# Exchanging softmax statistics between partitions on VectorE instead of GpSimd, in a fused linear attention and MLP kernel

## The chip, the cores and the metric

The kernel runs on one core of one Trainium2 chip. The metric is device time in microseconds (us) of one execution, as the median of several. A core has a matrix engine (TensorE, PE), with weight loads as a second stream (PEld), and VectorE (DVE), ScalarE (ACT) and GpSimd (POOL), each of which works through its own queue in order. SyncE (SP) issues most DMAs here. Engines wait for each other through semaphores only.

## The reference

Eight batches of eight heads, 576 positions, 64 features. The queries are softmaxed over their 64 features, the keys over their 576 positions; a head's output is `q_s @ (k_s^T @ v)`. The heads are then joined to tokens and go through an MLP without bias.

```python
q_s = exp(q - max(q, axis=-1));  q_s = q_s / (sum(q_s, axis=-1) + 1e-9)
k_s = exp(k - max(k, axis=2));   k_s = k_s / (sum(k_s, axis=2) + 1e-9)
kv  = einsum('bhsd,bhse->bhde', k_s, v)
x   = einsum('bhsd,bhde->bhse', q_s, kv)   # joined to 4608 tokens x 512
h   = x @ w_in                             # 512 -> 2048
out = (h * clip(h + 3, 0, 6) / 6) @ w_out  # 2048 -> 512
```

Inputs and output are float32; the two MLP weights come as float64.

## The kernel before, in words

The 4608 tokens are cut into nine blocks of 512 (`j` = 0 to 8). A block's 512 columns of `x` are made by four units, `attention(j, hp)`, one for each pair of heads. Then the block goes through the MLP, whose hidden dimension is cut into 16 slices of 128 (`f`). Almost every product is made as three matrix products of a rounded part (`hi`) and a rest (`lo`); `split` (L121 to L124) makes the two: ACT writes `hi` (L123), DVE the rest `lo` (L124). All matrix products carry the line of the helper `mm`, L91, and are told apart by their outputs: `ph` and `pz` the first MLP product, `po` the second, `px` the attention output, `pkv` the product of keys and values.

Blocks 0 and 1 run the first MLP product slice by slice (`gemm1`, then `gemm2`). Meanwhile the float64 weights are decoded to float32 (`decode`), and in block 1 sums and differences of weight blocks are made (`fast_weights`, L451 to L478) and stored to DRAM. From block 2 on, `fast_pair` makes two slices at once from seven smaller products with those sums, fetched again for every block. In it DVE and ACT read PSUM at L524 to L557; L554 adds the second PSUM tile, which the next pair's third product writes again. `x_factors` (L424) makes the matching sums of `x`; its four subtractions (L442 to L445) run on POOL, in the units of the second two head pairs.

An attention unit is a generator with four steps; the loops over `f` and over pairs call one step now and then, so that a block's attention is prepared while the block before is in the MLP. Step 1 loads the keys, values and queries and makes the softmax of the queries, for blocks 0 and 1 with `q_softmax`, from block 2 on with `q_softmax_t` (L292). Step 2 makes the exponentials of the keys (L353, L356) and splits the queries. Step 3 makes `pkv`, step 4 `px` and the factors.

In `q_softmax_t` a tile `qt` of 128 x 512 holds a pair of heads so that the 64 features of one head are two halves of 32, on two different groups of 32 partitions: partition group 0 has the first half of one head's features for 32 positions, group 1 the second half, groups 2 and 3 the same for the other head. Each row holds 16 groups of 32 features. A reduction along the row gives 16 statistics of half a softmax row (L297 the maximum, L301 the sum). `both_halves` joins the halves: it copies each group of 32 partitions of `stat` to its neighbour group in `swap` (four copies of 32 x 16, L289; `r ^ QD` is 0 to 32, 32 to 0, 64 to 96, 96 to 64) and combines `stat` with `swap` on DVE (L290). There are 28 units in blocks 2 to 8 with two statistics each, so 56 exchanges and 224 copies. Between and behind them: subtraction (L299, DVE), exponential (L300, ACT), `+ EPS` (L303), reciprocal (L304), scaling (L305) and a transpose in blocks of 32 x 32 (L307), all on DVE.

The order on PE is kept as written from block 1 on. The order on the other engines is not written out: a planner places instructions by priority and by when its own timeline model has them ready, on each engine's queue; `high_priority` raises the reads of PSUM. So moving an operation to another engine can change the order around it. `swap`, `qm` and `qr` have two buffers each.

POOL's other work is `decode`'s accumulating DMAs (L169, for the last six slices), the copy `kb` (L340) and L442 to L445.

Of the kernel before, what the change touches and what calls it, by code (L numbers as in the profile page):

```python
# [20 lines left out]
QD = 32  # L21
# [9 lines left out]
def attention_moe(  # L31
# [27 lines left out]
    nc = tc.nc  # L59
# [224 lines left out]
    def both_halves(stat, op):  # L284

        swap = att.tile([P, NG], F32, name="swap", bufs=2)
        for r in range(0, P, QD):
            o = r ^ QD
            nc.gpsimd.tensor_copy(swap[r : r + QD], stat[o : o + QD])  # L289
        nc.vector.tensor_tensor(stat, stat, swap, op=op)  # L290

    def q_softmax_t(qt):  # L292

        qs = qt.rearrange("p (g d) -> p g d", d=QD)
        qm = att.tile([P, NG], F32, name="qm", bufs=2)
        qr = att.tile([P, NG], F32, name="qr", bufs=2)
        nc.vector.tensor_reduce(qm, qs, axis=AX.X, op=ALU.max)  # L297
        both_halves(qm, ALU.max)
        nc.vector.tensor_sub(qs, qs, across(qm))  # L299
        nc.scalar.activation(qt, qt, AF.Exp)  # L300
        nc.vector.tensor_reduce(qr, qs, axis=AX.X, op=ALU.add)  # L301
        both_halves(qr, ALU.add)
        nc.vector.tensor_scalar_add(qr, qr, EPS)  # L303
        nc.vector.reciprocal(qr, qr)  # L304
        nc.vector.tensor_mul(qs, qs, across(qr))  # L305
        qT = moe.tile([P, 2 * DM], F32, name="m", tag="v", bufs=3)[:, 0:TB]
        nc.vector.transpose(qT, qt)  # L307
        return qT
# [465 lines left out]
```

## Time and profile before

| | |
|---|---|
| time, median of 3 runs | 892.73 us (892.33 to 893.6) |
| span of the profiled execution, first to last instruction | 888.9 us |
| PE busy | 858.4 us (97%) |
| DVE busy | 614.6 us (69%), 1266 instructions |
| ACT busy | 464.8 us (52%) |
| POOL busy | 132.9 us (15%), 329 instructions |
| of POOL, the 224 copies of L289 | 25.6 + 30.6 us |
| mean granted PE clock | 0.990 |

The profile is of one execution; the profiled one has its span, and no end-to-end time of its own is given. Busy time is the time in which at least one instruction of the engine ran. Rows of groups give the count, the busy time and the mean of one; rows of the timeline give start, duration, engine, line, operation, output and inputs, and in square brackets the engine's idle time before the instruction and what ended it. Pipelined instructions overlap, so that the start of the next can lie before the end of the one before.

### The profile page before, as it was taken

How to read it: one execution, taken by the hardware profiler on the slowest of the kernel's cores; microseconds unless marked ns; L12 is line 12 of the kernel's file. 1: busy time of each engine (PE TensorE's matmuls, PEld its weight loads, DVE VectorE, ACT ScalarE, POOL GpSimd, SP SyncE). 2: the span in 40 equal slices, each digit the busy share in tenths (PEclk: the TensorE clock that was granted, in tenths of full speed). 3: DMA queues.
4: the chain of work that ended last, by engine and by line, in shares of the span. 5: the costliest groups of instructions: out<-in, count | busy, mean ns of one | idle time of the engine just before them, and what ended most of it. 6: DMA issues, size and time to landing. Idle time of an engine off the chain costs nothing.

```text
span 888.9 us, 15262 instructions
## 1 busy us (share of the span) xinstructions
PE 858.4 (97%) x5380; PEld 739.2 (83%) x5380; DVE 614.6 (69%) x1266; ACT 464.8 (52%) x944; POOL 132.9 (15%) x329
## 2 busy tenths in 40 slices
PE   5799998999999999999999999999999999999998
PEld 3578776787789888888888888888888888889896
DVE  7999867899777766767585757676867565444333
ACT  7998753544445454545454545444554554434333
POOL 5000132021212110202020202021212120100000
PEclk9899999999999999999999999999999999999999
DMA  9992583538487668676777668676755575567541
GB/s 372 413 369 84 125 203 136 180 108 289 161 259 224 219 202 258 216 224 203 228 233 229 209 220 259 200 230 195 256 158 183 161 230 170 167 178 224 170 140 47
DMA packets 98474, 185.19 MB, mean 208 GB/s; under 512 B 9824, under 2 KB 24160, under 8 KB 96352
## 3 DMA queue, kind: packets, MB, share of 16 engines
q1 hardware_dynamic: 96192, 180.03, 62.3%
q0 software_dynamic: 1632, 3.15, 2.0%
q10 hardware_dynamic: 576, 1.05, 0.3%
q8 instruction: 43, 0.70, 0.3%
q14 instruction: 31, 0.25, 0.1%
HBM read 156.93 MB, written 24.12 MB: 204 GB/s over the span
## 4 chain that ended last, share of the span: by engine, by line
PE 83%; DVE 7%; DMA 6%; ACT 2%; issue 1%; POOL 0%; SPq 0%; ACTq 0%; DVEq 0%; POOLq 0%
PE po L91 41%; PE ph L91 33%; PE pz L91 4%; PE px L91 2%; PE pkv L91 2%; DMA w<-v 2%; DMA qt<-in_qf_dram 2%; DVE w L124 1%; DMA out_dram<-ob 1%; DVE v L155 1%; DVE v L149 0%; DMA wf<-w 0%; POOL swap L289 0%; DVE km L267 0%; DVE v L159 0%
## 5 line engine op out<-in xcount | busy, mean ns | idle before, releaser
L91 PE MATMUL po<-w,w 128*128 128x512 f32 x1008 | 260.8, 394 | 0.8 <-ACT w L123 0.8
L91 PEld LDWEIGHTS po<-w,w 128*128 128x128 f32 x1008 | 178.4, 189 | 30.7 <-ACT w L123 1.1
L91 PE MATMUL ph<-x_lo,w 128*128 128x256 f32 (+1 forms) x800 | 152.2, 305 | 2.7 <-DVE x_lo L124 2.3
L91 PEld LDWEIGHTS ph<-w,w 128*128 128x128 f32 x1008 | 133.8, 190 | 11.0 <-DVE second L535 1.4
L91 PE MATMUL ph<-x_hi,w 128*128 128x256 f32 (+1 forms) x592 | 138.4, 338 | 4.4 <-DMA w<-v 3.3
L91 PE MATMUL ph<-w,w 128*128 128x256 f32 x1008 | 140.4, 284 | 1.2 <-DVE second L535 1.2
L91 PEld LDWEIGHTS ph<-x_lo,w 128*128 128x128 f32 x800 | 117.0, 189 | 17.0 <-DVE x_lo L124 2.6
L91 PEld LDWEIGHTS ph<-x_hi,w 128*128 128x128 f32 x592 | 93.3, 191 | 18.8 <-DMA w<-v 3.5
L124 DVE TENSOR_TENSOR w<-g,w 128x512 fp32r<-128x512 f32 x112 | 77.2, 689 | 35.3 <-ACT w L123 35.3
L123 ACT CAST w<-g 128x512 fp32r<-128x512 f32 x112 | 69.4, 619 | 56.7 <-DVE g L541 34.4
L91 PE MATMUL po<-w 128*128 128x512 f32 x336 | 86.7, 394 | 0.1
L91 PEld LDWEIGHTS po<-w 128*128 128x128 f32 x336 | 59.4, 188 | 10.8 <-ACT w L123 0.5
L91 PE MATMUL po<-w,g_hi 128*128 128x512 f32 x256 | 67.4, 401 | 0.9 <-ACT g_hi L123 0.9
L556 ACT ACTIVATE g<-second,three 128x512 f32<-128x512 f32 x56 | 40.5, 724 | 33.9 <-DVE second L554 26.5
L91 PEld LDWEIGHTS po<-w,g_hi 128*128 128x128 f32 x256 | 47.7, 190 | 12.2 <-ACT g_hi L123 1.4
L540 ACT ACTIVATE g<-ph,three 128x256 f32<-128x256 f32 x56 | 26.6, 474 | 57.9 <-PE ph L91 57.9
L541 DVE SCALAR_TENSOR_TENSOR g<-g,ph 128x256 f32<-128x256 f32 x56 | 23.2, 415 | 47.1 <-ACT g L540 47.0
L534 ACT COPY second<-ph 128x256 f32<-128x256 f32 x56 | 20.8, 372 | 63.1 <-PE ph L91 63.1
L557 DVE SCALAR_TENSOR_TENSOR g<-g,second 128x512 f32<-128x512 f32 x56 | 39.0, 697 | 15.3 <-ACT g L556 15.2
L91 PE MATMUL pz<-x_hi,w 128*128 128x256 f32 x336 | 49.5, 283 | 0.0
L535 DVE TENSOR_TENSOR second<-second,ph 128x256 f32<-128x256 f32 x56 | 23.1, 413 | 37.5 <-ACT second L534 37.5
L289 POOL COPY swap<-qr 32x16 f32<-32x16 f32 x112 | 30.6, 273 | 96.4 <-DVE qr L301 92.8
(125 smaller groups left out, 1264.2 us busy)
## 6 DMA issues: line engine op xcount, KB each, us to landing
w<-wf SPq DMA_DIRECT2D x392, 256.0 KB, 3.0
raw<-in_w_dram SPq DMA_DIRECT2D x16, 1024.0 KB, 13.4
out_dram<-ob SPq DMA_DIRECT2D x36, 256.0 KB, 3.3
vt<-in_v_dram SPq DMA_DIRECT2D x28, 325.0 KB, 3.5
wf<-w SPq DMA_DIRECT2D x16, 512.0 KB, 4.7
kt<-in_kT_dram SPq DMA_DIRECT2D x28, 288.0 KB, 3.0
ke<-in_k_dram SPq DMA_DIRECT2D x24, 320.0 KB, 2.9
qt<-in_qf_dram SPq DMA_DIRECT2D x28, 256.0 KB, 3.0
```

The source lines that it names most:

```text
L91: nc.tensor.matmul(out, lhsT, rhs, start=start, stop=stop, skip_group_check=goes_on)
L123: nc.scalar.copy(hi, src)
L124: engine.tensor_sub(lo, src, hi.bitcast(F32))
L155: nc.vector.scalar_tensor_tensor(vu, high, 0xC0000000, m, op0=ALU.bitwise_and, op1=ALU.bitwise_or)
L289: nc.gpsimd.tensor_copy(swap[r : r + QD], stat[o : o + QD])
L534: nc.scalar.copy(second[:, HT:], x)
L535: nc.vector.tensor_add(second[:, HT:], second[:, HT:], y)
L540: nc.scalar.activation(r[:, HT:], x, AF.Relu, bias=three, scale=1.0)
L541: nc.vector.scalar_tensor_tensor(r[:, HT:], r[:, HT:], 6.0, x, op0=ALU.min, op1=ALU.mult)
L556: nc.scalar.activation(r, second, AF.Relu, bias=three, scale=1.0)
L557: nc.vector.scalar_tensor_tensor(r, r, 6.0, second, op0=ALU.min, op1=ALU.mult)
```

## The change

In `both_halves` the four copies are issued to VectorE's queue, where GpSimd's queue had them. Sizes, buffers and the operation after them are as they were. Blocks 0 and 1 don't use this function.

```diff
@@ def both_halves(stat, op):
         swap = att.tile([P, NG], F32, name="swap", bufs=2)
         for r in range(0, P, QD):
             o = r ^ QD
-            nc.gpsimd.tensor_copy(swap[r : r + QD], stat[o : o + QD])
+            nc.vector.tensor_copy(swap[r : r + QD], stat[o : o + QD])
         nc.vector.tensor_tensor(stat, stat, swap, op=op)
```

## The prediction

> **What bounds the kernel now.** First the page's busy times and its chain of waits by engine:
>
> ```profile
> PE 858.4 (97%) x5380; PEld 739.2 (83%) x5380; DVE 614.6 (69%) x1266; ACT 464.8 (52%) x944; POOL 132.9 (15%) x329
> PE 83%; DVE 7%; DMA 6%; ACT 2%; issue 1%; POOL 0%; SPq 0%; ACTq 0%; DVEq 0%; POOLq 0%
> ```
>
> TensorE (PE) works 858.4 of 888.9 us and fills 83% of the chain. A change on VectorE (DVE) and GpSimd (POOL) can only move the time where PE waits for DVE, or is made to. So the second view is time by stretch: PE, PE's weight loads, DVE, ACT and POOL busy, then the clock, the DMA share and GB/s.
>
> ```profile
> 133.00:144.00 11.00, 7.75 (x37) 5.54 (x34) 9.57 (x23) 3.86 (x7) 3.11 (x12) 1.00 0.58 190
> 165.00:225.00 60.00, 60.00 (x315) 48.22 (x314) 56.27 (x118) 31.00 (x58) 12.98 (x34) 1.00 0.58 187
> 580.00:592.00 12.00, 12.00 (x91) 10.52 (x91) 10.32 (x24) 6.28 (x12) 3.10 (x13) 1.00 0.68 216
> ```
>
> Three places matter: 133 to 144, where PE is idle for 3.25 us and DVE busy for 9.57; 165 to 225, where DVE is nearly full (56.27 of 60) but PE never stops; and the later blocks, of which 580 to 592 is a sample, with PE full and 1.68 us of DVE left. The third view is who waits for whom (us in total, times, longest), once for PE and once for the exchange:
>
> ```profile
> PE ph L91 <- DVE x_lo L124: 2.5, 2, 2.3
> ...
> DVE qr L290 <- POOL swap L289: 8.2, 15, 0.8
> ...
> DVE qm L290 <- POOL swap L289: 5.9, 15, 0.8
> ```
>
> DVE stands still 14.1 us in 30 waits for POOL's copies. PE's longest wait on DVE that lies near an exchange is the 2.3 us one, for x_lo.
>
> **The change, part by part.** Removed from POOL, and added to DVE:
>
> ```profile
> L289 POOL COPY swap<-qm x112: 186/192/693, 115.2 to 713.5; 32x16 f32<-32x16 f32 x112
> L289 POOL COPY swap<-qr x112: 186/192/1112, 122.8 to 716.7; 32x16 f32<-32x16 f32 x112
> L290 DVE TENSOR_TENSOR qm<-qm,swap x28: 113/174/177, 116.5 to 713.7; 128x16 f32<-128x16 f32 x28
> L290 DVE TENSOR_TENSOR qr<-qr,swap x28: 154/175/199, 124.6 to 717.4; 128x16 f32<-128x16 f32 x28
> ```
>
> These are 224 copies, four for each of 56 statistics (28 units of blocks 2 to 8, maximum and sum). On POOL their removal is worth nothing by itself: POOL is 15% busy. No DMA is moved. L169's accumulating DMAs are issued by POOL too, and no longer stand behind copies; the last of them, though, waited for ScalarE (ACT), not for a copy, and so gains nothing:
>
> ```profile
> 126.28 1.21 POOL L169 DMA_DIRECT2D w<-v x1 [1.70 <-ACT w L168]
> ```
>
> No row shows DVE copying 32 partitions of 16 elements. The nearest rows are DVE's operations on 128x16:
>
> ```profile
> 137.36 0.17 DVE L290 TENSOR_TENSOR qm<-qm,swap 128x16 f32<-128x16 f32 x1
> 137.45 0.15 DVE L216 RECIPROCAL rk<-rk 128x1 f32<-128x1 f32 x1
> ...
> 140.23 0.75 DVE L338 TENSOR_REDUCE km<-kt 128x1 f32<-128x576 f32 x1 [0.32 <-DMA kt<-in_kT_dram]
> 140.90 0.68 DVE L124 TENSOR_TENSOR g_lo<-g,g_hi 128x512 fp32r<-128x512 f32 x1
> 141.50 0.17 DVE L290 TENSOR_TENSOR qr<-qr,swap 128x16 f32<-128x16 f32 x1
> 142.13 0.17 DVE L290 TENSOR_TENSOR qm<-qm,swap 128x16 f32<-128x16 f32 x1 [0.47 <-POOL swap L289]
> ...
> 142.34 0.69 DVE L299 TENSOR_TENSOR qt<-qt,qm 128x512 f32<-128x512 f32 x1
> 142.95 0.68 DVE L124 TENSOR_TENSOR x_lo<-px,x_hi 128x512 fp32r<-128x512 f32 x1
> ```
>
> L216 starts 0.09 us after L290: small operations that don't depend on each other overlap. That is the low end, 4 x 0.09 = 0.36 us a statistic. The full 0.17 without overlap gives 0.68. A dependent step costs a little more; in this row pair it is 0.21 from L290 to L303:
>
> ```profile
> 222.43 0.17 DVE L290 TENSOR_TENSOR qr<-qr,swap 128x16 f32<-128x16 f32 x1 [0.33 <-POOL swap L289]
> 222.64 0.17 DVE L303 TENSOR_SCALAR qr<-qr 128x16 f32<-128x16 f32 x1
> ```
>
> So the high end is 4 x 0.21 = 0.84. I take 0.17 a copy, 0.68 a statistic: each copy changes the partitions that it reads and writes, which no overlapping pair here does. In all 56 x 0.68 = 38 us more on DVE, to about 653, against 14.1 us of its waits gone.
>
> The Trainium skill, in "VectorE: DVE Perf Modes" (Two Vector instructions with no wait between them), models a VectorE instruction as held until all earlier ones have finished when its start quadrant of 32 partitions differs from the one read or written last. All four copies change it, so by that rule each pays its full length, as in the value taken; by the overlapping row the addition would be 56 x 0.36 = 20 us. No run here shows the rule yet.
>
> *From 133 to 144 us.* Who was late is seen in PE's row and in ACT's, which made x_hi and with it released x_lo:
>
> ```profile
> 140.28 0.59 ACT L123 CAST x_hi<-px 128x512 fp32r<-128x512 f32 x1 [0.52 <-PE px L91]
> ...
> 143.69 0.51 PE L91 MATMUL ph<-x_lo,w 128*128 128x512 f32 x1 [2.27 <-DVE x_lo L124]
> ```
>
> x_lo could have started at 140.87 and started at 142.95, behind other work in DVE's queue, and PE waited 2.27 us. Three statistics are exchanged before it (the L290 rows at 137.36, 141.50 and 142.13). With the order kept, 12 copies at 0.17 are 2.04 us; the idle 0.47 (POOL) and 0.32 (the load of kt, which arrives meanwhile) absorb 0.79. Net +1.25 us, straight onto PE. The ends are 12 x 0.09 - 0.79 = +0.3 and 12 x 0.21 - 0.79 = +1.7. Below nothing: the order on DVE is set by a planner that places what is ready, and it may put x_lo at 140.87, which gives 2.08 us back.
>
> *From 165 to 225 us.* The exchange in this stretch:
>
> ```profile
> L290 DVE TENSOR_TENSOR qm<-qm,swap x3: 158/174/176, 174.9 to 217.0; 128x16 f32<-128x16 f32 x3
> L290 DVE TENSOR_TENSOR qr<-qr,swap x3: 156/175/176, 180.8 to 222.4; 128x16 f32<-128x16 f32 x3
> ...
> 228.29 0.69 DVE L297 TENSOR_REDUCE qm<-qt 128x16 f32<-128x512 f32 x1 [2.90 <-DMA qt<-in_qf_dram]
> ```
>
> Six statistics add 24 x 0.17 = 4.1 us to 60 - 56.27 = 3.73 us of idle DVE. DVE ends at most some tenths late, and its next idle time, 2.90 us before 228.29, takes that up. PE didn't wait once in 165 to 225, so I put it at 0; at 0.21 a copy the 1.3 us over would be the most.
>
> *The later blocks.* The rest of the exchange:
>
> ```profile
> L290 DVE TENSOR_TENSOR qm<-qm,swap x21: 113/174/177, 258.6 to 713.7; 128x16 f32<-128x16 f32 x21
> L290 DVE TENSOR_TENSOR qr<-qr,swap x21: 154/175/199, 267.4 to 717.4; 128x16 f32<-128x16 f32 x21
> ```
>
> These 42 statistics come in ten bunches of four (two units' preparation falls together) and one of two. One bunch, DVE's rows with idle time before them, and the PE group that needs L554's result (it writes the same bank again):
>
> ```profile
> 581.41 0.17 DVE L290 TENSOR_TENSOR qm<-qm,swap 128x16 f32<-128x16 f32 x1 [0.27 <-POOL swap L289]
> ...
> 583.21 0.69 DVE L297 TENSOR_REDUCE qm<-qt 128x16 f32<-128x512 f32 x1 [0.42 <-DMA qt<-in_qf_dram]
> ...
> 586.92 0.17 DVE L290 TENSOR_TENSOR qr<-qr,swap 128x16 f32<-128x16 f32 x1 [0.55 <-POOL swap L289]
> ...
> 591.21 0.69 DVE L301 TENSOR_REDUCE qr<-qt 128x16 f32<-128x512 f32 x1 [0.36 <-ACT qt L300]
> ...
> 593.27 0.17 DVE L290 TENSOR_TENSOR qr<-qr,swap 128x16 f32<-128x16 f32 x1 [0.51 <-POOL swap L289]
> 593.37 0.41 DVE L554 TENSOR_TENSOR second<-second,ph 128x256 f32<-128x256 f32 x1
> ...
> 594.60 1.59 PE L91 MATMUL ph<-w,w 128*128 128x256 f32 x12
> ```
>
> L554 ends at 593.78, 0.82 us before PE needs it. Before it lie 16 copies: 16 x 0.17 = 2.72, less the idle 0.27 + 0.42 + 0.55 + 0.36 + 0.51 = 2.11, so L554 comes 0.61 us later, inside the slack. PE sees 0. What hides it is this idle time and the slack; without the idle time, it would cost 2.72 - 0.82 = 1.9 us a bunch. The earliest thing to be late would be L554.
>
> **The sum.** +1.25 + 0 + 0 on the profiled execution's span of 888.9 gives 890.2. The span is 3.8 us below the median of the runs, 892.73; with the same 3.8 around it, 894.0 us. Less than 0.2% (1.8 us) is about what a measurement can't tell from no change, so this counts as "same".
>
> **The rivals.**
> *The bunches overflow (slower).* The mechanism is L554 behind the copies, and it decides once a statistic costs over (2.11 + 0.82) / 4 = 0.73 us. At 0.84, L554 is 3.36 - 2.11 - 0.82 = 0.43 us late in each of ten bunches, 4.3 us, with 1.7 in the first place: 892.73 + 6.0 = 898.7. For it: the copies depend on a reduction just before them, and DVE is 86% busy in the sample (10.32 of 12). Against it: this bunch is among the tight ones (PE is full there all the same), and high-priority reads of PSUM can be placed ahead of the copies.
>
> *The planner brings x_lo forward (faster).* Without the round trip to POOL, x_lo needs no place behind a stalled exchange. It gives back up to 2.27 us of PE's wait: 892.73 - 2.3 = 890.4. For it: x_lo was ready at 140.87. Against it: x_lo waited for 0.47 us of idleness only, the rest was other work, and now there is more of it.
>
> *Copies stand behind POOL's additions (slower).* These rows show a small DVE operation, of the kind with one tensor and a constant, held up while POOL works:
>
> ```profile
> 185.76 0.74 POOL L443 TENSOR_TENSOR v<-v 128x256 f32<-128x256 f32 x1
> ...
> 185.92 0.61 DVE L303 TENSOR_SCALAR qr<-qr 128x16 f32<-128x16 f32 x1
> ```
>
> L303 takes 0.61 us, 0.44 over its usual 0.17, and ends when POOL's addition does. Were the four copies of one statistic caught so in each of 14 units (two in each of seven blocks end in POOL's additions), 4 x 0.44 - 0.82 = 0.94 us each, that is 13 us, with the 1.25: 907 us. Against it: in the sampled bunch no such addition runs; the copies would have to move there.
>
> The Trainium skill, in "SBUF — State Buffer" (Who interferes with whom), says why: a VectorE copy in a two-port mode and a GpSimd operation lock each other out of a shared port pair for a whole instruction. The trace agrees in the row of 0.61 us.
>
> **Chances.** Forecast 0.43, bunches 0.26, port 0.09, planner 0.22. The forecast's time is 894.0. The range takes in the planner's 890.4 with a bit more and the bunches' 898.7, and leaves out the port: 889.6 to 899.5. Faster by over 0.2% is the planner's 0.22, slower the 0.26 + 0.09 = 0.35, same 0.43.
>
> **What would show each step.** L289 as 224 DVE copies with a spacing of 0.09, 0.17 or 0.21 us inside a group of four; DVE's busy time near 653 us (635 if they overlap) and no waits of L290 for POOL. PE's wait for x_lo near 3.5 us instead of 2.27 shows the first term; near 0 it is the planner's. PE busy all through 580 to 592 shows that the bunches are absorbed; a PE wait on L554 shows that they aren't. A copy of over 0.4 us beside a POOL addition shows the port. The forecast is wrong if PE's idle time after 165 us grows or shrinks by over 1 us, which would mean that DVE's order was changed far from the copies.

## The result, and the profile after

The changed kernel takes 903.4 us (900.53 to 905.38, six runs), against 892.28 us (891.38 to 893.6) of the kernel before in the same batch: ratio 1.0123, interval 1.0103 to 1.0142. That is 11 us slower, beyond the range given. The profiled execution has a span of 898.2 us, 9.3 more than before.

The page after, busy times and the chain by engine:

```profile
PE 863.7 (96%) x5380; PEld 739.4 (82%) x5380; DVE 649.0 (72%) x1490; ACT 463.0 (52%) x944; POOL 75.7 (8%) x105
PE 73%; DVE 15%; DMA 7%; ACT 2%; issue 2%; SPq 0%; ACTq 0%; DVEq 0%
```

DVE is busy for 649.0 us, 34.4 more than before, and its share of the chain went from 7% to 15%. The exchange itself, by its tile:

```profile
L289 DVE COPY swap<-qm x112: 161/166/171, 115.1 to 722.6; 32x16 f32<-32x16 f32 x112
L289 DVE COPY swap<-qr x112: 161/168/687, 125.2 to 727.3; 32x16 f32<-32x16 f32 x112
```

The copies have the price that was taken, 0.17 us, and some of the sum's take four times as long. L290 waits for nobody any more. The same three kinds of stretches as before (columns as in the prediction; the last is moved by 8 us, since the kernel is late there by that much):

```profile
133.00:144.00 11.00, 9.10 (x39) 6.30 (x36) 10.19 (x26) 3.42 (x8) 0.00 (x0) 0.91 0.54 171
165.00:225.00 60.00, 57.84 (x302) 45.80 (x300) 57.82 (x139) 27.95 (x52) 5.28 (x8) 1.00 0.56 185
588.00:600.00 12.00, 12.00 (x90) 10.45 (x89) 11.42 (x34) 5.63 (x11) 0.30 (x1) 1.00 0.64 189
```

The first got better, not worse (PE 9.10 of 11 us, part of it at a lower clock). In the second PE now stands still for 2.16 us, where it had not stopped. In the third DVE is nearly full, and PE still never stops. PE's waits after:

```profile
PE ph L91 <- DVE second L535: 2.8, 2, 1.7
...
PE px L91 <- ACT kv_hi L123: 1.9, 2, 1.5
...
PE ph L91 <- ACT x_hi L123: 1.7, 1, 1.7
...
PE ph L91 <- ACT first L524: 1.2, 4, 0.3
...
PE ph L91 <- DVE x_lo L124: 0.4, 2, 0.2
```

Where the 9.3 us come from is found by lining up the same matrix products in both traces, whose order on PE is nearly the same:

| a product that starts, before | after | late by | what lies between |
|---|---|---|---|
| 178.1 us | 178.2 us | 0.2 us | three exchanged units: nothing lost |
| 203.38 (po) | 205.66 | 2.3 | short waits: px at 184 and 203 us for kv_hi and kv_lo, pkv at 196 us for the keys |
| 221.59 (px for kv) | 225.51 | 3.9 | the longest wait, for kv_hi |
| 225.23 | 231.10 | 5.9 | a wait for kv_lo (4.3 us late then), then half clock |
| 241.1 | 246.1 | 5.0 | a wait of before (0.54 us, for g_hi) does not recur |
| 258.67 | 262.61 | 3.9 | half clock in the kernel before, none in the changed one |
| 278.63 | 284.28 | 5.7 | wait for L535 |
| 317.15 | 324.16 | 7.0 | first late L524 |
| 595.31 | 604.41 | 9.1 | the same in every second bunch |
| end | end | 9.3 | |

Two of the short waits in the changed kernel:

```profile
184.75 0.44 PE L91 MATMUL px<-qT_hi,kv_hi 128*128 128x384 f32 x1 [0.39 <-ACT kv_hi L123]
...
197.80 0.95 PE L91 MATMUL pkv<-vt,ke 128*64 128x65 f32 x20 [0.64 <-ACT ke L356]
```

So 4.3 us are lost by waiting up to px's last product at 222 us, half of it before the longest wait; some 2 us more come near 280 us and 3 us in four later bunches. The clock cancels in this pair: the changed kernel loses about 1.5 us by it behind px, the kernel before as much from 254.59 us.

**The px wait.** The order on DVE in the changed kernel, from the factor rk to kv_lo, with PE's pkv, which rk needs, ahead of it:

```profile
217.00 0.95 PE L91 MATMUL pkv<-vt,ke 128*64 128x65 f32 x20
...
220.38 0.15 DVE L215 TENSOR_SCALAR rk<-pkv 128x1 f32<-128x1 f32 x1
220.45 0.68 DVE L301 TENSOR_REDUCE qr<-qt 128x16 f32<-128x512 f32 x1
...
221.71 0.15 DVE L216 RECIPROCAL rk<-rk 128x1 f32<-128x1 f32 x1
221.90 0.16 DVE L289 COPY swap<-qr 32x16 f32<-32x16 f32 x1
222.08 0.69 DVE L124 TENSOR_TENSOR g_lo<-g,g_hi 128x512 fp32r<-128x512 f32 x1
222.78 0.53 DVE L289 COPY swap<-qr 32x16 f32<-32x16 f32 x3
...
223.68 0.34 DVE L218 SCALAR_TENSOR_TENSOR kv<-pkv,rk,mask 128x128 f32<-128x128 f32 x1
...
224.65 0.61 ACT L123 CAST w<-ob 128x512 fp32r<-128x512 f32 x1
225.16 0.30 ACT L123 CAST kv_hi<-kv 128x128 fp32r<-128x128 f32 x1
...
225.51 0.44 PE L91 MATMUL px<-qT_hi,kv_hi 128*128 128x384 f32 x1 [1.49 <-ACT kv_hi L123]
226.47 0.44 PE L91 MATMUL px<-qT_hi,kv_lo 128*128 128x384 f32 x1 [0.35 <-DVE kv_lo L124]
```

And the same place before:

```profile
214.72 0.95 PE L91 MATMUL pkv<-vt,ke 128*64 128x65 f32 x20
...
220.04 0.34 DVE L218 SCALAR_TENSOR_TENSOR kv<-pkv,rk,mask 128x128 f32<-128x128 f32 x1
...
220.64 0.67 DVE L301 TENSOR_REDUCE qr<-qt 128x16 f32<-128x512 f32 x1
...
220.41 0.30 ACT L123 CAST kv_hi<-kv 128x128 fp32r<-128x128 f32 x1 [0.62 <-DVE kv L218]
...
221.59 0.39 PE L91 MATMUL px<-qT_hi,kv_hi 128*128 128x384 f32 x1
```

Before, L301 (the sum of another unit) came behind L218, and kv_hi was ready 0.88 us before px needed it. Now L301 and the four copies of its sum stand between L215 and L218; L218 ends only at 224.02, 6.07 us after the end of pkv, where it took 4.71 us before. By then ScalarE's queue has gone on to the weight sums (`w<-ob`), and kv_hi runs behind them, 1.1 us later behind L218 than before. The two delays, 1.36 and 1.1 us, less the 0.88 us of slack make the 1.6 us that px loses here. PE waits for 1.49 and 0.35 us. None of this depends on the exchange that causes it: it belongs to a unit of the next block.

**The clock behind it.** The three windows of 3.41 us around that pause, in the changed kernel:

```profile
223.87:227.28 3.41, 1.57 (x8) 1.03 (x8) 3.11 (x9) 2.54 (x6) 0.00 (x0) 1.00 0.52 167
227.28:230.69 3.41, 3.41 (x10) 2.63 (x9) 0.00 (x0) 2.50 (x7) 2.11 (x3) 0.50 0.98 343
230.69:234.11 3.42, 3.42 (x16) 2.77 (x15) 3.25 (x10) 0.00 (x0) 0.00 (x0) 1.00 0.08 30
```

PE is idle for 1.84 us in the first, and in the second it is granted half the clock and does 10 products instead of about 16. The kernel before has the same at another place, behind a wait of its own for L535:

```profile
251.18:254.59 3.41, 1.73 (x12) 1.40 (x12) 2.03 (x5) 1.50 (x4) 0.00 (x0) 1.00 0.88 249
254.59:258.00 3.41, 3.41 (x18) 3.31 (x17) 2.86 (x8) 1.91 (x4) 1.77 (x5) 0.50 0.76 238
```

**The first bunch.** Near 281 us the sum's copies lie beside GpSimd's additions, and the read of PSUM behind them makes PE wait:

```profile
280.48 1.20 POOL L444 TENSOR_TENSOR v<-v 128x256 f32<-128x256 f32 x1
281.62 0.74 POOL L445 TENSOR_TENSOR v<-v 128x256 f32<-128x256 f32 x1
...
281.08 1.68 DVE L289 COPY swap<-qr 32x16 f32<-32x16 f32 x4
283.82 0.41 DVE L535 TENSOR_TENSOR second<-second,ph 128x256 f32<-128x256 f32 x1
...
284.28 0.97 PE L91 MATMUL ph<-w,w 128*128 128x256 f32 x6 [1.11 <-DVE second L535]
```

Four copies take 1.68 us here and about 0.70 elsewhere.

**The later bunches.** In every second one L554 is late, then ScalarE's L556, which waits for it, and L524 behind that:

```profile
322.41 0.42 DVE L554 TENSOR_TENSOR second<-second,ph 128x256 f32<-128x256 f32 x1
...
322.93 0.72 ACT L556 ACTIVATE g<-second,three 128x512 f32<-128x512 f32 x1 [2.22 <-DVE second L554]
323.75 0.36 ACT L524 COPY first<-ph 128x256 f32<-128x256 f32 x1
...
324.16 0.98 PE L91 MATMUL ph<-w,w 128*128 128x256 f32 x6 [0.29 <-ACT first L524]
```

Before, the two groups of six products here ran as one; now the first starts some 0.27 us late and the second another 0.46 us, 0.73 us in all.

### The profile page after: what moved, and what is told of

Same layout as the page of the kernel before. It is cut to its first block, busy times and chain, and to the rows that moved or that the text cites. A ratio compares the mean times of both kernels' runs of the same rounds, so it can differ in the third digit from the quotient of the medians.

```text
span 898.2 us, 15191 instructions
## 1 busy us (share of the span) xinstructions
PE 863.7 (96%) x5380; PEld 739.4 (82%) x5380; DVE 649.0 (72%) x1490; ACT 463.0 (52%) x944; POOL 75.7 (8%) x105
## 4 chain that ended last, share of the span: by engine, by line
PE 73%; DVE 15%; DMA 7%; ACT 2%; issue 2%; SPq 0%; ACTq 0%; DVEq 0%
PE po L91 36%; PE ph L91 29%; PE pz L91 4%; PE px L91 2%; DVE w L124 2%; PE pkv L91 2%; DMA qt<-in_qf_dram 2%; DMA kt<-in_kT_dram 2%; DVE swap L289 1%; DMA w<-wf 1%; DMA w<-v 1%; DMA out_dram<-ob 1%; DVE v L155 1%; DVE km L338 1%; DVE g L573 1%
## 5 line engine op out<-in xcount | busy, mean ns | idle before, releaser
L91 PEld LDWEIGHTS po<-w,w 128*128 128x128 f32 x1008 | 178.1, 188 | 30.7 <-ACT w L123 1.1
L91 PE MATMUL po<-w,g_hi 128*128 128x512 f32 x256 | 69.2, 409 | 0.4 <-ACT g_hi L123 0.4
L556 ACT ACTIVATE g<-second,three 128x512 f32<-128x512 f32 x56 | 40.5, 724 | 39.1 <-DVE second L554 29.9
L535 DVE TENSOR_TENSOR second<-second,ph 128x256 f32<-128x256 f32 x56 | 23.1, 413 | 37.2 <-ACT second L534 37.2
L91 PEld LDWEIGHTS pz<-x_hi,w 128*128 128x128 f32 x336 | 43.8, 188 | 0.1
```

The costliest lines, as they stand in the source:

```text
L91: nc.tensor.matmul(out, lhsT, rhs, start=start, stop=stop, skip_group_check=goes_on)
L535: nc.vector.tensor_add(second[:, HT:], second[:, HT:], y)
L556: nc.scalar.activation(r, second, AF.Relu, bias=three, scale=1.0)
```

## The experiments

All times are set against the kernel before on the same chip, whose median was 891.4 to 892.8 us in the batches.

**By block.** The engine was made an argument of `both_halves` and chosen by block:

```diff
-            nc.vector.tensor_copy(swap[r : r + QD], stat[o : o + QD])
+            engine.tensor_copy(swap[r : r + QD], stat[o : o + QD])
...
-            qT = q_softmax_t(qt)
+            qT = q_softmax_t(qt, nc.vector if j == 2 else nc.gpsimd)   # e1_block2
+            qT = q_softmax_t(qt, nc.vector if j > 2 else nc.gpsimd)    # e2_later
```

> VectorE's copies in block 2 alone (its four units are prepared while block 1 is in the MLP), GpSimd's in blocks 3 to 8. Theory 1 (the loss is made where VectorE is already full, 165 to 245 us: there the new queue makes px wait for kv, and a PE pause costs a window of half clock on top): about half of the 11 us, 897 us (895.5 to 899). Theory 2 (the loss is made in the later blocks, where ten bunches of exchanges run over their slack): 892 to 894 us.

Measured: 891.97 us, ratio 1.0002 (0.9988 to 1.0016).

> The other half: GpSimd's copies in block 2, VectorE's in blocks 3 to 8. Theory 1: what is left of the loss, about 4 to 5 us, 896 to 898 us, of which 1.5 us at the first bunch and about 0.8 in every second bunch. Theory 2: all of it, 901 to 904 us. If the two halves add up to far less or far more than 11 us, the loss is one of the order as a whole and not of places.

Measured: 898.29 us, ratio 1.0088 (1.0066 to 1.0109). Block 2 alone costs nothing, so theory 1 had the place right and the block wrong: the units whose exchange begins from 182 us on are already block 3's. In the trace of the second kernel the px wait of 1.49 us is there, 1.11 us at the first bunch and four late L524. The two parts, +0.0002 and +0.0088, add up to less than the whole, +0.0123; against the +0.0106 of the second measurement below the difference is within the intervals.

**Copies that nobody reads.** GpSimd makes the exchange, and VectorE copies the same data into a tile of its own:

```diff
             nc.gpsimd.tensor_copy(swap[r : r + QD], stat[o : o + QD])
+            nc.vector.tensor_copy(spare_swap[r : r + QD], stat[o : o + QD])
```

> The kernel before, with GpSimd's exchange kept, and beside it the same four copies on VectorE into a tile that nobody reads: VectorE's time and queue slots without a change in who makes the exchange. If the price is VectorE's occupancy (4 x 0.18 us a statistic in a queue that PE waits for), 899 to 904 us. If it is the place of the copies in the chain of the softmax (reduction, copies, combination all on one queue), the dummy copies can run at any time and the time stays within 2 us of before, 891 to 895 us.

Measured: 898.35 us, ratio 1.0079 (1.0051 to 1.0108), DVE busy 650.0 us. The time lies between the two ranges, nearer to the first. Most of the loss is there although GpSimd makes the exchange: slots in VectorE's queue, and the order that is planned around them, are enough. The copies are not as free as the expectation has it, though: L290 overwrites `stat`, which they read, so they too stand between the reduction and L290, and the run doesn't separate their slots from their place in the chain. The px wait is 1.49 us here as well.

**Priority for the kv steps.** Around L215 to L218 and the split of kv:

```diff
+        with tc.high_priority():
             rk = att.tile([P, 1], F32, name="rk", bufs=2)
             nc.vector.tensor_scalar_add(rk, pkv[:, D : D + 1], EPS)
...
+        with tc.high_priority():
             split(*kvs[j, hp], kv)
```

> The changed kernel with high priority for the six VectorE and ScalarE operations that make kv out of pkv and split it. If px's waits for kv (1.49 and 0.39 us) and the half clock after the longer one are a matter of queue order, they go: about 3 to 4 us less than the changed kernel, 899 to 900 us. If VectorE's time itself is short there, the wait turns up at another operation and the time stays at 902 to 905 us.

Measured: 900.43 us, ratio 1.0110 (1.0089 to 1.0130), near the first range, but the px wait is unchanged:

```profile
226.35 0.44 PE L91 MATMUL px<-qT_hi,kv_hi 128*128 128x384 f32 x1 [1.49 <-ACT kv_hi L123]
```

The half clock behind it is absent in this execution. Priority did not move these steps, so the run says nothing on what moving them would bring.

**By statistic.** `both_halves(qm, ...)` on VectorE and `both_halves(qr, ...)` on GpSimd, and the reverse, with the engine as an argument as above.

> VectorE's copies for the maximum alone (112 of 224), GpSimd's for the sum. Theory Sum (the copies of the sum do the harm: they stand in VectorE's queue ahead of the steps that make kv and beside GpSimd's additions): close to before, 891 to 893.5 us. Theory Load (any 112 copies of 0.18 us on VectorE cost about half): 896 to 898 us.

Measured: 892.84 us, ratio 1.0001 (0.9986 to 1.0017).

> The other half: VectorE's copies for the sum, GpSimd's for the maximum. Theory Sum: most of the loss, 899 to 903 us, with px's wait of about 1.5 us for kv near 224 us in its trace. Theory Load: 896 to 898 us.

Measured: 891.37 us, ratio 0.9992 (0.9973 to 1.0012). Either half is free, and both together cost 11 us: both theories fall. In the second kernel VectorE's copies were held at the first bunch even longer than in the changed kernel, and PE waited:

```profile
273.51 2.12 DVE L289 COPY swap<-qr 32x16 f32<-32x16 f32 x3
...
278.20 0.98 PE L91 MATMUL ph<-w,w 128*128 128x256 f32 x6 [1.06 <-DVE second L535]
```

With the maximum alone no copy took over 0.25 us, and PE's longest wait for L535 was 0.5 us. So the port costs about 1 us at that place, which the total of this kernel does not show.

**ScalarE.** The four copies as `nc.scalar.copy`:

> All 224 copies on ScalarE, which is busy 52%. If the loss is VectorE's queue alone, the time comes back to 890 to 893 us, and may fall below before since VectorE no longer waits 14 us for GpSimd. If a short copy on any engine that reads PSUM for PE costs PE time by its place in the queue, 895 to 902 us.

Measured: 899.08 us, ratio 1.0090 (1.0059 to 1.0120). The copies take 0.20 us each there and stand ahead of the splits of the MLP's activations:

```profile
352.19 0.84 ACT L289 COPY swap<-qm 32x16 f32<-32x16 f32 x4
353.06 0.62 ACT L123 CAST w<-g 128x512 fp32r<-128x512 f32 x1
...
353.73 1.18 PE L91 MATMUL po<-w,w 128*128 128x512 f32 x4 [2.18 <-ACT w L123]
```

The second alternative came true: a half-idle engine (57% busy here) that PE waits for is no place for them either.

**Weight sums on GpSimd.** In the changed kernel:

```diff
-            nc.vector.tensor_add(
+            nc.gpsimd.tensor_add(
                 whole[:, at : at + TB], src[:, 0].bitcast(F32), src[:, 1].bitcast(F32)
             )
```

> The changed kernel with the 16 additions of the weights' two parts (L459, 128x512, 0.67 us each on VectorE) moved to GpSimd, now nearly idle: this takes some 10 us from VectorE between 133 and 232 us, more than the exchange adds there. Theory Load: px's waits for kv shrink and the time falls by 3 to 5 us against the changed kernel, 898 to 900 us. Theory Order (the planner's places for the copies, whatever VectorE's load): px still waits near 224 us, 902 to 905 us. GpSimd and VectorE may also hold each other up, which would add to it.

Measured: 905.1 us, ratio 1.0166 (1.0130 to 1.0203). VectorE is not less busy (651.3 us): the additions take 1.44 us on GpSimd, and copies beside them wait. In its trace px's wait for kv_hi shrinks to 0.54 us, as Theory Load had it, but pkv waits for the keys for 1.46 us and the time rises. The run therefore doesn't decide between its theories.

```profile
243.04 2.83 DVE L289 COPY swap<-qr 32x16 f32<-32x16 f32 x4
```

**The changed kernel again.**

> The changed kernel unaltered, for a second trace beside the others: 901 to 905 us. The same places as before should be late: px near 224 us by about 1.5 us, the first bunch near 283 us by about 1.1 us, and steps of 0.7 us in every second bunch.

Measured: 901.66 us, ratio 1.0106 (1.0083 to 1.0128). The waits are the same (px 1.49, L535 1.11, L524 0.29 us in four bunches), with a span of 898.8 us; only the half clock behind px is missing.

**The sum's half in step 2.**

```diff
         nc.scalar.activation(qt, qt, AF.Exp)
+        yield
         nc.vector.tensor_reduce(qr, qs, axis=AX.X, op=ALU.add)
...
-            qT = q_softmax_t(qt)
+            qs = q_softmax_t(qt)
+            next(qs)
         yield
+        if not early:
+            qT = next(qs)
```

> The changed kernel with the second half of the queries' softmax (sum, its exchange, reciprocal, scaling, transpose) given to the unit's step 2 instead of step 1: the same 224 copies on VectorE, in other places. Theory Order (where the planner puts the sum's exchange decides): 892 to 897 us. Theory Load (four statistics in a bunch overflow wherever they stand): 900 to 905 us.

Measured: 909.04 us, ratio 1.0181 (1.0163 to 1.0200). The same 224 copies in another order lose 7 us more; px alone waits for 3.1 us at once:

```profile
PE px L91 <- ACT kv_hi L123: 3.1, 1, 3.1
```

It is the order, not only the number, but not in the direction expected; and the edit moves the whole second half of the softmax, not the copies alone.

**Two and three of four copies on VectorE.**

```diff
+            engine = nc.vector if r < 2 * QD else nc.gpsimd   # e11_two_two; 3 * QD in e12_three_one
+            engine.tensor_copy(swap[r : r + QD], stat[o : o + QD])
```

> Of each statistic's four copies two on VectorE and two on GpSimd: 112 on VectorE, as many as in the two kernels with one statistic each on VectorE, but spread over all exchanges. Theory Threshold (a bunch of four statistics takes eight copies of 0.18 us in its idle time, and sixteen not): 890 to 894 us. Theory Both (each exchange that has a copy on VectorE is late): 896 to 900 us.

Measured: 894.07 us, ratio 1.0019 (1.0002 to 1.0035).

> Three copies on VectorE and one on GpSimd: 168 on VectorE. Theory Threshold: twelve copies a bunch are 2.1 us, just the idle time of 2.11 us found in the bunch of 580 to 594 us, so 893 to 898 us, between the two ends. Theory Order: no relation to the number, anywhere from 891 to 905 us.

Measured: 895.99 us, ratio 1.0035 (1.0016 to 1.0053). Both are at or inside the threshold's ranges (894.07 at the edge of 890 to 894); the second is inside that of Theory Order as well, which it therefore doesn't exclude.

**Without block 3, and without its first unit.** The engine was chosen by `nc.gpsimd if j == 3 else nc.vector`, and with `and hp == 0` in the condition.

> The changed kernel with GpSimd's copies in the four units of block 3 alone (the first is prepared from 182 to 240 us, the others in the first bunches), 192 copies on VectorE. Theory Place (block 3's exchange makes the px wait, the half clock behind it and the late first bunch, some 6 us; what stays are the small steps of the later bunches): 894 to 897 us, and no px wait of 1.49 us near 224 us. Theory Number (only how many copies VectorE has counts): as the other kernel with 192 copies, 898 us or more.

Measured: 897.78 us, ratio 1.0064 (1.0045 to 1.0084), between the two ranges. The px wait is gone, as Theory Place had it; at the first bunch 0.65 us for L535 are left.

> The same for the first unit of block 3 alone: 8 copies on GpSimd, 216 on VectorE. Its sum is exchanged between 182 and 188 us, and the copies near 222 us are the second unit's. If the px wait near 224 us hangs on those, it stays at 1.49 us and the time falls by 1 us at most, to 901 to 904 us. If it hangs on VectorE's load since 180 us, it shrinks to under 1 us and the time falls by 2 to 3 us, to 899 to 901 us.

Measured: 897.76 us, ratio 1.0073 (1.0048 to 1.0098). That is below both ranges. Eight copies fewer on VectorE take off about as much as 32 (the two intervals overlap), and the px wait is gone in both. In the second kernel:

```profile
221.66 0.35 DVE L218 SCALAR_TENSOR_TENSOR kv<-pkv,rk,mask 128x128 f32<-128x128 f32 x1
...
222.25 0.68 DVE L301 TENSOR_REDUCE qr<-qt 128x16 f32<-128x512 f32 x1
...
223.75 0.70 DVE L289 COPY swap<-qr 32x16 f32<-32x16 f32 x4
...
223.09 0.39 PE L91 MATMUL px<-qT_hi,kv_hi 128*128 128x384 f32 x1
```

The second unit's copies are still on VectorE, but L301 and they come behind L218 once more, as in the kernel before, and PE doesn't wait. VectorE is no less busy for it: over the same 398 products, which start at 165 us and end at 241 us before, it is busy for 72.31 us, against 72.05 in the changed kernel and 67.37 before, and the kernel is 2.0 us late at their end instead of 5.0. What remains are 1.08 us at the first bunch and the late L524.

| copies on VectorE | which | ratio to before |
|---|---|---|
| 32 | block 2 | 1.0002 |
| 112 | maximum; sum; two of four | 1.0001; 0.9992; 1.0019 |
| 168 | three of four | 1.0035 |
| 192 | without block 2; without block 3 | 1.0088; 1.0064 |
| 216 | without block 3's first unit | 1.0073 |
| 224 | all; all, again; all, sum in step 2 | 1.0123; 1.0106; 1.0181 |
| 224 | all, kv steps raised; all, weight sums on GpSimd | 1.0110; 1.0166 |
| 224 unread | GpSimd exchanges | 1.0079 |

## Why the prediction was wrong, point by point

- *What bounds the kernel, and where DVE touches it.* Right as far as it went. PE sets the end, and the loss is PE's waiting; the half clock behind it cancels against that of the kernel before, and the second execution of the changed kernel, with half clock at neither place, is late by 9.9 us all the same.
- *The price of a copy, 0.17 us.* Right: 0.166 to 0.168 us median, four in about 0.70 us with no overlap. DVE's busy time is 649 us, forecast about 653. With the Trainium skill's rule of held instructions ("VectorE: DVE Perf Modes", Two Vector instructions with no wait between them) the trace agrees.
- *133 to 144 us, +1.25.* Wrong in sign. The planner did move x_lo forward (PE's wait 2.27 to 0.17 us), as the faster rival had it; the product ahead of it then waited longer for x_hi (0.68 to 1.73 us). The product that had waited starts 1.0 us earlier than before (142.67 against 143.69), and a window of half clock from 142 us, which the kernel before doesn't have there, takes that back: 0.2 us late at 146 and at 178 us, a term of about 0.
- *165 to 225 us, put at 0.* This is the step that failed. It compared VectorE's added time with its idle time (4.1 against 3.73 us) and took PE's not waiting for slack. The slack that counted was that of one chain: kv_hi was ready 0.88 us before px, and kv_lo hardly before its use. The copies, and the sum ahead of them, went in between L215 and L218 (1.36 us), and ScalarE's queue added 1.1 us. Measured: 2.0 us there, after 2.1 us of short waits for kv and the keys between 178 and 204 us: 4.3 us of lateness in all.
- *The later blocks, put at 0, with 0.43 us a bunch at the high price.* The place was right (L554), the slack was not. It was reckoned to PE's use of PSUM through L554 alone; the chain through ScalarE's L556 and L524 to the next product was left out. Measured: 0.73 us in every second bunch, over four bunches 2.9 us.
- *The port.* The mechanism was right and its place was missed: in the changed kernel six copies of 224 took over 0.25 us, four of them in two units beside the additions, and one of these units made PE wait for 1.11 us. The rival had priced it at 14 units.
- *The order.* The forecast named the planner as a source of gain only. That a longer queue makes it place another unit's exchange ahead of an urgent step was not among the cases. The sign that the forecast named for it came: PE's idle time in 165 to 225 us grew from 0 to 2.16 us.

What the runs settle: VectorE's total load doesn't set the loss (without block 3's first unit VectorE is as busy over the same products and 3 us less are lost there), and the exchange need not be made on VectorE for most of it to appear. At px it is shown that the order decides: with L301 and the copies behind L218 the wait is gone. For the short waits and the later bunches that is argued from the trace of the changed kernel. What stays open: whether copies that could run at any time would cost as much, why the planner puts L301 ahead of L218 in some of these kernels, how much of the loss that of its order is and how much would remain with the order of before and all copies on VectorE (no run had that), and how the smaller late steps in 184 to 200 us divide.

## What to carry to other kernels

When work moves to an engine that other engines wait for, compare it with the slack of each chain that runs through its queue, up to the last consumer and through the next engine's queue, not with the engine's idle time. Taking eight copies of 0.17 us back brought as much here as taking 32 back, since another unit's work then stood behind one urgent step again. Where a planner sets the order, any move re-plans the neighbours: test it in parts, by block and by operand, since halves that are free can cost 1% together.

## What the runs showed of the hardware

- A pause of PE can cost more than its length. In the changed kernel PE was busy for 1.57 of the 3.41 us before 227.28 us, and was then granted half the clock for 3.41 us, which cost 1.5 us. In the second execution the same pause of 1.49 us was not followed by half clock: there the windows, in step with that trace's own changes of clock, ended at 224.72 and 228.13 us, and PE was busy for 2.72 and 2.40 us of them. The Trainium skill ("TensorE: Matmul & The Clock Gate", What's actually happening) describes windows of 3413 ns that run freely, which fits the pause falling differently into them; it has the clock fall after a window of idleness, and here a window in which PE was busy for 46% was enough. Over all 16 traces of this case, after their first 48 us and in windows in step with each trace's changes of clock, the full clock always gave way to half behind windows with PE busy for up to 1.64 us, never behind those with over 1.95, and now and then in between.
- A VectorE copy of 16 elements a partition beside a GpSimd addition takes as long as what is left of the addition: 0.61 to 0.69 us here beside additions of 0.74 to 1.20 us, and 2.83 us for four beside those of 1.44 us, against 0.17 alone. The Trainium skill's exclusive port pair ("SBUF — State Buffer", Who interferes with whom) says the same.
